# Retention and PReLU MLP on one core: masked scores with q^T, and v with the carried sums, as one product of 128 rows and 64 columns

## The chip, the cores and the metric

The kernel runs on one core of a Trainium2 chip. The metric is the device time of one execution in microseconds. Before the change the median of three runs is 1047.41 us (1045.88 to 1048.51). A profiled execution, which all durations below come from, took 1043.84 us, and its span from the first to the last instruction is 1042.1 us, at a mean granted TensorE clock of 0.997.

## What is computed

Two blocks follow each other. The first is retention: for 8 batches, 8 heads, 576 positions and 64 values a head,

```python
scores = scale * np.matmul(q, k.transpose(0, 1, 3, 2))
gamma = 1.0 - 2.0 ** (-5.0 - np.arange(H, dtype=np.float32))
Dmat = np.where(rel >= 0, gamma[:, None, None] ** rel[None, :, :], 0.0)
ret = scores * Dmat[None, :, :, :]
return np.matmul(ret, v).astype(np.float32)
```

where `rel` is the query's position minus the key's. The result is read as 4608 tokens of 512 values and goes through an MLP, `h = x @ w_in` (512 x 2048), `g = max(h, 0) + alpha * min(h, 0)`, `g @ w_out` (2048 x 512). All data are fp32.

## The kernel before, in words

**Retention in chunks.** The 576 positions of a head are cut into nine chunks of C = 64. A query of chunk j meets the keys of its own chunk through masked scores, and all earlier chunks through one carried sum, a 64x64 matrix of k^T v with its decay. The powers of gamma are put into q and v ahead of the products, so that the mask is only a triangle of ones and a factor for each head. Heads are worked in pairs (c = 0 to 3 in each batch, index n = 4b + c), two heads to the 128 partitions.

For each pair four steps are run, each a function:

- `transposes` (L528): GpSimd multiplies q by its table (L534) and v by its own (`scale`, L512, whose line is L515), and VectorE turns k and q into kT and qT of 64 rows a head, by transposes of 32x32 squares (L539), whose loads `load_sq` lays out so that whole heads come out turned.
- `scores` (L564): 20 products of 64x64 (L573), one head in each half of the rows. VectorE multiplies them by mask and factor (L577) into `at`, in which chunk 2m lies in the lower 64 partitions and chunk 2m + 1 in the upper.
- `states` (L582): 16 products of 64x64 (L588) give k^T v of each chunk but the last; ScalarE copies the even ones (L593), and VectorE adds up the carried sums `su` (L594, L597, L599).
- `values` (L606): 18 products of 64x64 of v with `at` (L612), and 32 of 64 rows by 32 columns of `su` with qT (L619), accumulated in the same PSUM banks. `put_x` (L491) copies the result into the MLP's input blocks with ScalarE (L503, L505); odd chunks lie in exchanged halves and take two copies for each.

**The MLP.** Tokens come in 18 blocks of 256 (kb), the inner dimension in eight slices (i); a pair (kb, i) is a unit. From block 2 on, each unit uses seven products of halves in place of eight: `combine_x` (L420, GpSimd, L427) makes differences of the input, `mlp_unit` (L429) does 14 products of 128x128 by 128 columns (L441); ScalarE copies one of them (L447), VectorE adds (L452), applies the activation (L455, L457) and makes the differences for the second layer (L463); `mlp_out` (L353) does seven products of 256 columns (L361) one unit later. After the last slice `out_block` (L335) adds up the output on VectorE (L347, L348) and stores it.

**Order.** Batch 0 is done in a stage written out by hand while weights are loaded and reduced, batch 1 in the gaps of MLP blocks 0 and 1, whose products are plain (L397, L376). From the third batch on (n = 8 to 31, 24 pairs) the loop at L895 runs `scores`, `states`, the transposes of the next pair and `values`, with units of the queue between them: `cuts` spreads 16 or 24 queued units over the four pairs of a batch, so 4 or 6 go with each pair. One unit lies between states and values in five of the six batches, two in the other. Here the framework's scheduler orders each engine's instructions; each engine runs its own queue in order. The loads of pair n + 1 are issued from SyncE at the start of pair n. Tiles of k, q and v (`nat`) have two buffers each; `kT`, `at` have one, `qT` and `su` two. The products of retention share two PSUM banks (`ps_a`), those of the MLP have two (`ps_h`) and four (`ps_o`).

Of the kernel before, what the change touches and what calls it, by code (L numbers as in the profile page):

```python
# [18 lines left out]
def kernel(  # L19
# [46 lines left out]

    pairs = [(b, c) for b in range(B) for c in range(NPAIR)]

    NEARLY = 2 * NPAIR
# [3 lines left out]
    def load_nat(t, src, b, c):  # L75
        hs, s0 = slice(2 * c, 2 * c + 2), (NM - 1) * P
        for h2 in range(2):
            nc.sync.dma_start(t[:, 0:NM - 1, h2],
                              src[b, 2 * c + h2, 0:s0].rearrange("(m p) d -> p m d", p=P))
        nc.sync.dma_start(t[0:C, NM - 1], src[b, hs, s0:S].rearrange("h p d -> p h d"))  # L80
# [3 lines left out]
    def load_sq(t, src, b, c):  # L84
        for a in range(4):
            f0 = (a % 2) * 32
            nc.sync.dma_start(
                t[32 * a:32 * a + 32],
                src[b, 2 * c + a // 2].rearrange("(n t) d -> t n d", t=32)[:, :, f0:f0 + 32])

    def load_pair(n):
        b, c = pairs[n]
        kn, vn, qx = [nat.tile([P, NM, 2, D], FP32, tag=f"nat_{x}", name=f"{x}n_{n}")
                      for x in "kvq"]
        if n < NEARLY:
            kx = kn
            load_nat(kn, k, b, c)
            load_nat(qx, q, b, c)
        else:
            kx = nat.tile([P, NB, 32], FP32, tag="sq_k", name=f"kx_{n}")  # L100
            qx = qx.rearrange("p m h d -> p (m h d)")[:, 0:S].rearrange(
                "p (n r) -> p n r", r=32)
            load_sq(kx, k, b, c)
            load_sq(qx, q, b, c)
            load_nat(kn, k, b, c)
        load_nat(vn, v, b, c)
        return kn, kx, qx, vn


# [99 lines left out]

    gch = const.tile([P, 3, NPAIR], FP32, name="gch")  # L210
    tabx = const.tile([P, NPAIR, 2], FP32, name="tabx")
    for h2 in range(2):
        hd = slice(h2 * D, (h2 + 1) * D)
        nc.vector.tensor_copy(gch[hd, 0], th[hd, 2, h2:H:2])
        nc.vector.tensor_scalar(tabx[hd, :, 0], pf[hd, 0, h2:H:2], float(D) ** -0.5, None,
                                ALU.mult)
        nc.vector.scalar_tensor_tensor(out=tabx[hd, :, 1], in0=dif[hd, 5, h2:H:2], scalar=1.0,
                                       in1=tabx[hd, :, 0], op0=ALU.add, op1=ALU.mult)
# [301 lines left out]
    def ps_tile(shape, name):  # L520
        return ps_a.tile(shape, FP32, tag="psa", name=name)
# [6 lines left out]
    def transposes(n):  # L528
        c = pairs[n][1]
        kn, kx, qx, vn = loaded[n]  # L530
        kT = attn.tile([P, S], FP32, tag="kT", name=f"kT_{n}")
        qT = attn.tile([P, S], FP32, tag="qT", bufs=2, name=f"qT_{n}")
        qh = qx.rearrange("p (j x) r -> p j x r", x=2)
        nc.gpsimd.tensor_tensor(out=qh, in0=qh,  # L534
                                in1=tabx[:, None, c, :, None].to_broadcast([P, NJ, 2, 32]),
                                op=ALU.mult)
        scale(vn, 1, c)
        for src, dst in ((kx, kT), (qx, qT)):
            nc.vector.transpose(dst, src.rearrange("p n r -> p (n r)"))  # L539
        return kT, qT  # L540

    def turn(n, i):

        src = loaded[n][i]
        dst = attn.tile([P, S], FP32, tag="qT" if i else "kT", bufs=2 if i else 1,
                        name=f"T{i}_{n}")
        for m0, m1 in ((0, 3), (3, NM)):
            w = min(m1 * P, S) - m0 * P
            pt = ps_tile([P, 3 * P], f"pt{i + m0}_{n}")
            for m in range(m0, m1):  # L550
                rows = min(P, S - m * P)
                nc.tensor.transpose(pt[:, (m - m0) * P:(m - m0) * P + rows],  # L552
                                    src[0:rows, m].rearrange("p h d -> p (h d)"),
                                    ident[0:rows, 0:rows])
            nc.scalar.copy(dst[:, m0 * P:m0 * P + w], pt[:, 0:w])
        return dst

    def half(x):
        return slice(x * C, (x + 1) * C)

    def chunk(j):
        return slice(j * C, (j + 1) * C)

    def scores(n, kT, qT):  # L564
        c = pairs[n][1]
        at = attn.tile([P, 2 * NM * C], FP32, tag="at", name=f"at_{n}").rearrange(
            "p (h m s) -> h p m s", h=2, s=C)
        ps = [ps_tile([P, NM, C], f"ps{h2}_{n}") for h2 in range(2)]
        for m in range(NM):
            for p2 in range(2):  # L570
                j = min(2 * m + p2, NJ - 1)
                for h2 in range(2):
                    nc.tensor.matmul(ps[h2][half(p2), m], kT[half(h2), chunk(j)],  # L573
                                     qT[half(h2), chunk(j)], start=True, stop=True)
        for h2 in range(2):
            h = 2 * c + h2
            nc.vector.scalar_tensor_tensor(  # L577
                out=at[h2], in0=ps[h2], scalar=th[:, 3, h:h + 1],
                in1=mask[:, None, :].to_broadcast([P, NM, C]), op0=ALU.mult, op1=ALU.mult)
        return at  # L580

    def states(n, kn, vn):  # L582
        c = pairs[n][1]
        ps = [ps_tile([P, NM - 1, D], f"pu{p2}_{n}") for p2 in range(2)]
        for m in range(NM - 1):
            for p2 in range(2):
                for h2 in range(2):
                    nc.tensor.matmul(ps[p2][half(h2), m], kn[half(p2), m, h2],  # L588
                                     vn[half(p2), m, h2], start=(m == 0), stop=(m == NM - 2),
                                     skip_group_check=True)  # L590
        su = attn.tile([P, NJ - 1, D], FP32, tag="su", bufs=2, name=f"su_{n}")
        g1, g2 = gch[:, 0, c:c + 1], gch[:, 1, c:c + 1]
        nc.scalar.copy(su[:, 0::2], ps[0])  # L593
        nc.vector.scalar_tensor_tensor(out=su[:, 1::2], in0=su[:, 0::2], scalar=g1, in1=ps[1],  # L594
                                       op0=ALU.mult, op1=ALU.add)
        for j in range(3, NJ - 1, 2):
            nc.vector.scalar_tensor_tensor(out=su[:, j], in0=su[:, j - 2], scalar=g2,  # L597
                                           in1=su[:, j], op0=ALU.mult, op1=ALU.add)
        nc.vector.scalar_tensor_tensor(out=su[:, 2::2], in0=su[:, 1:NJ - 3:2], scalar=g1,  # L599
                                       in1=ps[0][:, 1:], op0=ALU.mult, op1=ALU.add)  # L600
        return su
# [4 lines left out]
    def values(n, vn, qT, at, su):  # L606
        b, c = pairs[n]
        pv = [ps_tile([P, NM, C], f"pv{p2}_{n}") for p2 in range(2)]
        for m in range(NM):
            for p2 in range(2 if 2 * m + 1 < NJ else 1):  # L610
                for h2 in range(2):
                    nc.tensor.matmul(pv[p2][half(h2 ^ p2), m], vn[half(p2), m, h2],  # L612
                                     at[h2][half(p2), m], start=(m == 0), stop=False,
                                     skip_group_check=True)
        for j in range(1, NJ):
            for h2 in range(2):
                for e in range(0, D, 32):
                    to = (h2 ^ (j % 2)) * D + e
                    nc.tensor.matmul(pv[j % 2][to:to + 32, j // 2],  # L619
                                     su[half(h2), j - 1, e:e + 32], qT[half(h2), chunk(j)],  # L620
                                     start=False, stop=(j >= NJ - 2), skip_group_check=True)
        for p2 in range(2):
            put_x(b, c, p2, pv[p2])

# [268 lines left out]
    for n, (b, c) in enumerate(pairs):  # L895
        if n < NEARLY:
            continue
        if n + 1 < len(pairs):
            loaded[n + 1] = load_pair(n + 1)
        kn, _, _, vn = loaded[n]  # L900
        share = -(-len(queue) // (NPAIR - c))
        cuts = [(share + i) // 3 for i in range(3)][::-1]
        kT, qT = turned.pop(n) if n in turned else transposes(n)
        at = scores(n, kT, qT)
        pop_units(cuts[0])
        su = states(n, kn, vn)
        pop_units(cuts[1])
        if n + 1 < len(pairs):
            turned[n + 1] = transposes(n + 1)
        values(n, vn, qT, at, su)  # L910
        del loaded[n]
        pop_units(cuts[2])
        if c == NPAIR - 1:
            enqueue(b)
# [31 lines left out]
```

## Time and profile before

| What | from the profile |
|---|---|
| span | 1042.1 us |
| DMA, mean busy share of 16 engines, in tenths | 9 in the first fortieth of the span, 0 to 8 in the next nine, then 1 to 3, 0 in the last eight |
| scores of a pair (L573) | 40 records, mean 223 ns each, overlapped |
| states of a pair (L588) | 32 records, mean 224 ns |
| values of a pair (L612, L619) | 36 records, 223 ns, and 64 records, 224 ns |
| MLP, first layer (L441) | 3584 records, 275 and 278 ns |
| MLP, second layer (L361) | 1792 records, 379 ns |

A record of a matmul is one pass: each fp32 product shows as two passes in the trace, so the 20 products of `scores` are 40 records. The mean duration of a record says how long one pass is in the array, from its first row to its end; passes overlap, so the time that a group takes is read from the chain of work that ended last, not from the mean. A few matmul records can be missing from a trace. In the groups, "64*32" after a name is the part of the array that the product used, rows by columns.

### The profile page before, as it was taken

The numbers are of one execution on the slowest core, as the hardware profiler recorded it, in microseconds if no ns is written. First come the engines' busy times: TensorE is split into PE (matmuls) and PEld (weight loads), VectorE is DVE, ScalarE is ACT, GpSimd is POOL, SyncE is SP. The second block draws the span as 40 slices with busy tenths as digits, with TensorE's granted clock in tenths as the row PEclk, the third lists the DMA queues.
The fourth block names the chain that finished last, engine by engine and source line by source line (L and its number), as shares of the span: only waits on it lengthen the run. The fifth ranks groups of instructions, "written<-read, shape, count | busy, mean of one in ns | idle before, by whom it ended". The sixth has DMA issues, their size and how long they took to land.

```text
span 1042.1 us, 27067 instructions
## 1 busy us (share of the span) xinstructions
PE 1024.3 (98%) x11329; PEld 902.0 (87%) x11329; DVE 748.2 (72%) x1951; ACT 170.8 (16%) x533; POOL 214.8 (21%) x253
## 2 busy tenths in 40 slices
PE   5999999999999999999999999999999999999998
PEld 4766667999999999999999999999999999999997
DVE  7766755776786778776768777867777776766675
ACT  4545532111111110110110011111111111000000
POOL 4566675411301020200011111301030001010000
PEclk8999999999999999999999999999999999999999
DMA  9855605233232221121212232222222100000000
GB/s 244 252 153 139 163 20 122 41 68 64 48 67 45 59 47 44 35 56 24 56 36 50 42 68 46 57 47 53 62 40 52 24 22 2 21 1 22 1 21 21
DMA packets 216073, 63.36 MB, mean 61 GB/s; under 512 B 201088, under 2 KB 209296, under 8 KB 215952
## 3 DMA queue, kind: packets, MB, share of 16 engines
q1 hardware_dynamic: 213840, 61.11, 25.3%
q8 instruction: 89, 1.46, 0.6%
q10 hardware_dynamic: 2112, 0.53, 0.3%
q14 instruction: 32, 0.26, 0.1%
HBM read 52.17 MB, written 9.44 MB: 59 GB/s over the span
## 4 chain that ended last, share of the span: by engine, by line
PE 97%; DMA 1%; issue 1%; POOL 0%; DVE 0%; ACT 0%; SPq 0%; DVEq 0%; POOLq 0%
PE ph L441 40%; PE po L361 37%; PE ph L397 6%; PE po L376 5%; PE pv L619 2%; PE ps L573 2%; PE pv L612 2%; PE pu L588 2%; DMA w_out<-in_k_dram 1%; PE pt L552 0%; PE pt L653 0%; PE pv L726 0%; PE ps L672 0%; PE pv L715 0%; POOL w_out L304 0%
## 5 line engine op out<-in xcount | busy, mean ns | idle before, releaser
L361 PE MATMUL po<-w_out,g 128*128 128x256 f32 x1792 | 407.8, 379 | 0.0
L361 PEld LDWEIGHTS po<-w_out,g 128*128 128x128 f32 x1792 | 330.8, 190 | 39.7
L452 DVE TENSOR_TENSOR g<-ph,g 128x256 f32<-128x256 f32 (+1 forms) x512 | 187.4, 387 | 176.6 <-PE ph L441 95.7
L441 PE MATMUL ph<-xb,w_in 128*128 128x128 f32 x2048 | 277.6, 278 | 0.0
L441 PEld LDWEIGHTS ph<-xb,w_in 128*128 128x128 f32 x2048 | 253.2, 192 | 9.2 <-issue 0.7
L441 PE MATMUL ph<-xt,w_in 128*128 128x128 f32 x1536 | 213.6, 275 | 0.0
L441 PEld LDWEIGHTS ph<-xt,w_in 128*128 128x128 f32 x1536 | 192.2, 192 | 0.1
L463 DVE TENSOR_TENSOR g<-g 128x128 f32<-128x128 f32 x512 | 143.0, 320 | 7.8
L447 ACT COPY g<-ph 128x128 f32<-128x128 f32 x128 | 34.0, 265 | 462.2 <-PE ph L441 457.3
L515 POOL TENSOR_TENSOR vn<-vn,th 128x512 f32<-128x512 f32 (+1 forms) x56 | 39.7, 729 | 336.0 <-DMA vn<-in_v_dram 315.2
L455 DVE TENSOR_SCALAR g<-g,alpha 128x256 f32<-128x256 f32 x256 | 92.1, 402 | 4.5
L457 DVE SCALAR_TENSOR_TENSOR g<-g 128x512 f32<-128x512 f32 x128 | 91.8, 717 | 3.8
L397 PE MATMUL ph<-xb,w_in 128*128 128x256 f32 x256 | 61.1, 394 | 1.1 <-ACT xb L733 1.1
L427 POOL TENSOR_TENSOR xt<-xb,xt 128x256 f32<-128x256 f32 x32 | 25.2, 788 | 172.3 <-ACT xb L505 163.3
L376 PE MATMUL po<-w_out,g 128*128 128x512 f32 x128 | 59.0, 604 | 0.1
L397 PEld LDWEIGHTS ph<-xb,w_in 128*128 128x128 f32 x256 | 49.2, 196 | 10.0 <-issue 2.4
L503 ACT COPY xb<-pv 64x64 f32<-64x64 f32 (+1 forms) x144 | 33.9, 236 | 145.7 <-PE pv L619 143.9
L376 PEld LDWEIGHTS po<-w_out,g 128*128 128x128 f32 x128 | 23.1, 190 | 24.3 <-issue 22.5
L539 DVE STREAM_TRANSPOSE qT<-qn 128x576 f32<-128x576 f32 x24 | 18.7, 778 | 28.9 <-PE pv L619 23.1
L413 DVE SCALAR_TENSOR_TENSOR g<-g,nalpha,ph 128x256 f32<-128x256 f32 x32 | 13.9, 477 | 31.6 <-ACT ph L403 31.6
L534 POOL TENSOR_TENSOR qn<-qn,tabx 128x576 f32<-128x576 f32 x24 | 28.1, 1171 | 28.7 <-DMA qn<-in_q_dram 22.8
L427 POOL TENSOR_TENSOR xt<-xb 128x256 f32<-128x256 f32 x16 | 11.5, 722 | 107.3 <-PE ph L441 107.3
(127 smaller groups left out, 665.0 us busy)
## 6 DMA issues: line engine op xcount, KB each, us to landing
out_dram<-osb SPq DMA_DIRECT2D x36, 256.0 KB, 2.2
kn<-in_k_dram SPq DMA_DIRECT2D x56, 128.0 KB, 2.9
vn<-in_v_dram SPq DMA_DIRECT2D x56, 128.0 KB, 2.8
kx<-in_k_dram SPq DMA_DIRECT2D x96, 72.0 KB, 2.5
qn<-in_q_dram SPq DMA_DIRECT2D x96, 72.0 KB, 2.6
raw<-in_moe_w_in_dram SPq DMA_DIRECT2D x24, 256.0 KB, 4.2
raw<-in_moe_w_out_dram SPq DMA_DIRECT2D x10, 512.0 KB, 4.5
w_in<-in_moe_w_out_dram SPq DMA_DIRECT2D x6, 512.0 KB, 4.8
```

What stands on the lines that cost most here:

```text
L361: nc.tensor.matmul(acc[kb][n // 2][:, n % 2, :], g[:, x, :], w_out[i][:, y, :], start=(i == 0 and n % 2 == 0), stop=(i == NU - 1 and (n % ...
L376: nc.tensor.matmul(acc[kb][m], g[:, 2 * x + m], w_out[i][:, 2 * x:2 * x + 2].rearrange("p x f -> p (x f)"), start=(i == 0 and x == 0), sto ...
L397: nc.tensor.matmul(ph[:, x], w_in[i // UST][:, cc // 2 * 2 + x, i % UST, cc % 2], xb[kb][:, cc], start=(cc == 0 and x == 0), stop=(cc == N ...
L427: nc.gpsimd.tensor_tensor(out=o, in0=x0, in1=x1, op=ALU.subtract)
L441: nc.tensor.matmul(ph[m][:, o], w_in[i // UST][:, l, i % UST, cc], r[:, cc], start=(n in (0, 3) and cc == 0), stop=(n in (2, 6) and cc == ...
L447: nc.scalar.copy(g[:, 7], ph[0][:, 2])
L452: nc.vector.tensor_tensor(out=o, in0=x0, in1=x1, op=ALU.add)
L455: nc.vector.tensor_scalar(g[:, 4 + 2 * m:6 + 2 * m], g[:, 2 * m:2 * m + 2], 0.0, alpha[:, fc:fc + 1], ALU.min, ALU.mult)
L457: nc.vector.scalar_tensor_tensor(out=g[:, 0:4].rearrange("p x t -> p (x t)"), in0=g[:, 0:4].rearrange("p x t -> p (x t)"), scalar=0.0, in1 ...
L463: ins = nc.vector.tensor_tensor(out=g[:, o, :], in0=g[:, x0, :], in1=g[:, x1, :], op=op)
L503: nc.scalar.copy(to[half(h2)], pv[half(1 - h2), m:m + n])
L515: nc.gpsimd.tensor_tensor(out=t[0:rows, m], in0=t[0:rows, m], in1=th[0:rows, x, None, 2 * c:2 * c + 2, None].to_broadcast([rows, n, 2, D]) ...
```

## The change

From the third batch on, v and the carried sums of a head are put into one matrix of 128 rows for each chunk, and the masked scores and q^T into another, so that one product gives a chunk's values of one head. In the tile of v, head h2 has v in the partitions of the other half (`half(1 - h2)`) and the carried sums in its own half; the first chunk has zeros there, set by GpSimd. In the tile `mt`, head h2 has masked scores in the other half and its q^T in its own. So `pair_values` has 18 products of 128 rows, 64 columns of the array and 64 columns of data, without accumulation, and head h2 comes out in the half of the PSUM partitions that it has in the MLP's input. ScalarE copies q^T into `mt` and the sums into v's tile, and it now multiplies v by its table, which GpSimd did. `pair_scores` has 18 products in place of 20, its mask takes four operations of 64 partitions, `pair_states` has two for the odd sums. The functions `scores`, `states` and `values` stay for the pairs of batch 1.

Besides, k (as the states need it) and v are loaded with the positions of a chunk in 64 partitions, two loads each in place of three; the sums of the new pairs lie in kT's buffer, those of batch 1 in that of k's squares; qT has one buffer; and the transposes of pair 8 come ahead of the loads of pair 9 and behind one MLP unit, which leaves 15 of the 16 units to that batch's `cuts`. The core of the diff:

```diff
     def load_pair(n):
...
-            load_nat(kn, k, b, c)
-        load_nat(vn, v, b, c)
+            kn = kn[:, 0:S].rearrange("p (j d) -> p j d", d=D)
+            vn = vn.rearrange("p (h j d) -> p h j d", h=2, d=D)
+            for h2 in range(2):
+                load_head(kn[half(1 - h2)], k, b, 2 * c + h2)
+                load_head(vn[half(1 - h2), h2], v, b, 2 * c + h2)
+
+                nc.gpsimd.memset(vn[half(h2), h2, 0], 0.0)
...
     def transposes(n):
...
-        qT = attn.tile([P, S], FP32, tag="qT", bufs=2, name=f"qT_{n}")
+        qT = attn.tile([P, S], FP32, tag="qT", name=f"qT_{n}")
...
-        scale(vn, 1, c)
+        for h2 in range(2):
+            x = half(1 - h2)
+            nc.scalar.activation(vn[x, h2], vn[x, h2], ACTF.Copy, scale=tabv[x, c:c + 1])
...
     def states(n, kn, vn):
...
-        su = attn.tile([P, NJ - 1, D], FP32, tag="su", bufs=2, name=f"su_{n}")
+        su = nat.tile([P, S], FP32, tag="sq_k", name=f"su_{n}")[:, 0:S - D].rearrange(
+            "p (j d) -> p j d", d=D)
...
+    def pair_scores(n, kT, qT):
...
+        ps = [ps_tile([P, NM, C], f"ps{p2}_{n}") for p2 in range(2)]
+        for j in range(NJ):
+            for h2 in range(2):
+                x = (1 - h2, h2)[j % 2]
+                nc.tensor.matmul(ps[j % 2][half(x), j // 2], kT[half(h2), chunk(j)],
+                                 qT[half(h2), chunk(j)], start=True, stop=True)
+        for h2 in range(2):
+            nc.scalar.copy(mt[half(h2), h2].rearrange("p j s -> p (j s)"), qT[half(h2)])
+        for p2 in range(2):
+            for h2 in range(2):
+                h, to, x = 2 * c + h2, half(1 - h2), (1 - h2, h2)[p2]
+                nm = NM - p2
+                nc.vector.scalar_tensor_tensor(
+                    out=mt[to, h2, p2::2], in0=ps[p2][half(x), 0:nm], scalar=th[to, 3, h:h + 1],
+                    in1=mask[to, None, :].to_broadcast([C, nm, C]), op0=ALU.mult, op1=ALU.mult)
+        return mt
+
+    def pair_states(n, kn, vn):
...
+        su = attn.tile([P, S], FP32, tag="kT", name=f"su_{n}")[:, 0:S - D].rearrange(
+            "p (j d) -> p j d", d=D)
+        g1, g2 = gch[:, 0, c:c + 1], gch[:, 1, c:c + 1]
+        nc.scalar.copy(su[:, 0::2], ps[0])
+        for h2 in range(2):
+            nc.vector.scalar_tensor_tensor(
+                out=su[half(h2), 1::2], in0=su[half(h2), 0::2], scalar=g1[half(h2)],
+                in1=ps[1][half(1 - h2)], op0=ALU.mult, op1=ALU.add)
...
+        for h2 in range(2):
+            nc.scalar.copy(vn[half(h2), h2, 1:], su[half(h2)])
+
+    def pair_values(n, vn, mt):
...
+        j1 = -b * NJ % w or w
+        j1 += w if NJ - j1 > 6 else 0
+        pv = [ps_tile([P, (j1, NJ - j1)[i], C], f"pv{i}_{n}") for i in range(2)]
+        for j in range(NJ):
+            for h2 in range(2):
+                nc.tensor.matmul(pv[j >= j1][half(h2), j - (j1 if j >= j1 else 0)],
+                                 vn[:, h2, j], mt[:, h2, j], start=True, stop=True)
...
+            m, i = min(w - o, NJ - j), j >= j1
+            j0 = j - (j1 if i else 0)
+            nc.scalar.copy(xb[kb][:, c, o * C:(o + m) * C].rearrange("p (j s) -> p j s", s=C),
+                           pv[i][:, j0:j0 + m])
...
+        if n == NEARLY:
+            pop_units(1)
+            turned[n] = transposes(n)
         if n + 1 < len(pairs):
             loaded[n + 1] = load_pair(n + 1)
...
-        kT, qT = turned.pop(n) if n in turned else transposes(n)
-        at = scores(n, kT, qT)
+        kT, qT = turned.pop(n)
+        mt = pair_scores(n, kT, qT)
         pop_units(cuts[0])
-        su = states(n, kn, vn)
+        pair_states(n, kn, vn)
         pop_units(cuts[1])
         if n + 1 < len(pairs):
             turned[n + 1] = transposes(n + 1)
-        values(n, vn, qT, at, su)
+        pair_values(n, vn, mt)
```

More of the change, by code (lines that the diff above doesn't have):

```diff
@@ L67, with half @@
     pairs = [(b, c) for b in range(B) for c in range(NPAIR)]
+    def half(x):
+        return slice(x * C, (x + 1) * C)
     NEARLY = 2 * NPAIR
@@ L89, in load_sq, with load_head @@
                 src[b, 2 * c + a // 2].rearrange("(n t) d -> t n d", t=32)[:, :, f0:f0 + 32])
+    def load_head(t, src, b, h):
+        nc.sync.dma_start(t, src[b, h].rearrange("(j t) d -> t j d", t=C))
     def load_pair(n):
         b, c = pairs[n]
-        kn, vn, qx = [nat.tile([P, NM, 2, D], FP32, tag=f"nat_{x}", name=f"{x}n_{n}")
-                      for x in "kvq"]
+        kn = nat.tile([P, NM * P], FP32, tag="nat_k", name=f"kn_{n}")
+        qx = nat.tile([P, NM * P], FP32, tag="nat_q", name=f"qn_{n}")
+        vn = nat.tile([P, 2 * S], FP32, tag="nat_v", name=f"vn_{n}")
         if n < NEARLY:
+            kn, qx, vn = [t[:, 0:NM * P].rearrange("p (m h d) -> p m h d", h=2, d=D)
+                          for t in (kn, qx, vn)]
             kx = kn
@@ L98, in load_pair @@
             load_nat(qx, q, b, c)
+            load_nat(vn, v, b, c)
         else:
-            kx = nat.tile([P, NB, 32], FP32, tag="sq_k", name=f"kx_{n}")
-            qx = qx.rearrange("p m h d -> p (m h d)")[:, 0:S].rearrange(
+            kx = nat.tile([P, S], FP32, tag="sq_k", name=f"kx_{n}").rearrange(
                 "p (n r) -> p n r", r=32)
+            qx = qx[:, 0:S].rearrange("p (n r) -> p n r", r=32)
             load_sq(kx, k, b, c)
             load_sq(qx, q, b, c)
-            load_nat(kn, k, b, c)
-        load_nat(vn, v, b, c)
+            kn = kn[:, 0:S].rearrange("p (j d) -> p j d", d=D)
[4 more added lines that the diff above has]
+                nc.gpsimd.memset(vn[half(h2), h2, 0], 0.0)
         return kn, kx, qx, vn
@@ L211 @@
     tabx = const.tile([P, NPAIR, 2], FP32, name="tabx")
+    tabv = const.tile([P, NPAIR], FP32, name="tabv")
     for h2 in range(2):
         hd = slice(h2 * D, (h2 + 1) * D)
+        nc.vector.tensor_copy(tabv[half(1 - h2)], th[half(1 - h2), 1, h2:H:2])
         nc.vector.tensor_copy(gch[hd, 0], th[hd, 2, h2:H:2])
@@ L544, in turn @@
         src = loaded[n][i]
-        dst = attn.tile([P, S], FP32, tag="qT" if i else "kT", bufs=2 if i else 1,
-                        name=f"T{i}_{n}")
+        dst = attn.tile([P, S], FP32, tag="qT" if i else "kT", name=f"T{i}_{n}")
         for m0, m1 in ((0, 3), (3, NM)):
@@ L556, in turn @@
         return dst
-    def half(x):
-        return slice(x * C, (x + 1) * C)
     def chunk(j):
@@ L565, in scores @@
         c = pairs[n][1]
-        at = attn.tile([P, 2 * NM * C], FP32, tag="at", name=f"at_{n}").rearrange(
+        at = attn.tile([P, 2 * S], FP32, tag="at", name=f"at_{n}")[:, 0:2 * NM * C].rearrange(
             "p (h m s) -> h p m s", h=2, s=C)
@@ L623, in values @@
             put_x(b, c, p2, pv[p2])
+    def pair_scores(n, kT, qT):
+        c = pairs[n][1]
+        mt = attn.tile([P, 2 * S], FP32, tag="at", name=f"mt_{n}").rearrange(
+            "p (h j s) -> p h j s", h=2, s=C)
+        ps = [ps_tile([P, NM, C], f"ps{p2}_{n}") for p2 in range(2)]
[14 more added lines that the diff above has]
+        return mt
@@ new lines, in pair_states @@
+    def pair_states(n, kn, vn):
+        c = pairs[n][1]
+        ps = [ps_tile([P, NM - 1, D], f"pu{p2}_{n}") for p2 in range(2)]
+        for j in range(NJ - 1):
+            for h2 in range(2):
+                x = (h2, 1 - h2)[j % 2]
+                nc.tensor.matmul(ps[j % 2][half(x), j // 2], kn[half(1 - h2), j],
+                                 vn[half(1 - h2), h2, j], start=True, stop=True)
+        su = attn.tile([P, S], FP32, tag="kT", name=f"su_{n}")[:, 0:S - D].rearrange(
[6 more added lines that the diff above has]
+                in1=ps[1][half(1 - h2)], op0=ALU.mult, op1=ALU.add)
+        for j in range(3, NJ - 1, 2):
+            nc.vector.scalar_tensor_tensor(out=su[:, j], in0=su[:, j - 2], scalar=g2,
+                                           in1=su[:, j], op0=ALU.mult, op1=ALU.add)
+        nc.vector.scalar_tensor_tensor(out=su[:, 2::2], in0=su[:, 1:NJ - 3:2], scalar=g1,
+                                       in1=ps[0][:, 1:], op0=ALU.mult, op1=ALU.add)
+        for h2 in range(2):
+            nc.scalar.copy(vn[half(h2), h2, 1:], su[half(h2)])
@@ new lines, in pair_values @@
+    def pair_values(n, vn, mt):
+        b, c = pairs[n]
+        w = TB // C
+        j1 = -b * NJ % w or w
+        j1 += w if NJ - j1 > 6 else 0
+        pv = [ps_tile([P, (j1, NJ - j1)[i], C], f"pv{i}_{n}") for i in range(2)]
+        for j in range(NJ):
+            for h2 in range(2):
+                nc.tensor.matmul(pv[j >= j1][half(h2), j - (j1 if j >= j1 else 0)],
+                                 vn[:, h2, j], mt[:, h2, j], start=True, stop=True)
+        j = 0
+        while j < NJ:
+            kb, o = divmod(b * NJ + j, w)
+            if kb not in xb:
+                xb[kb] = ring.tile([P, NCC, TB], FP32, tag=f"x{kb % NRING}", name=f"xb_{kb}")
+            m, i = min(w - o, NJ - j), j >= j1
+            j0 = j - (j1 if i else 0)
+            nc.scalar.copy(xb[kb][:, c, o * C:(o + m) * C].rearrange("p (j s) -> p j s", s=C),
+                           pv[i][:, j0:j0 + m])
+            j += m
```

## The prediction

> **What bounds the kernel now.** I read the busy shares first, then who ended the waits of TensorE, then the chain that ended last. The busy shares (the columns are busy time, share of the span, instructions):
>
> ```profile
> PE 1024.3 (98%) x11329; PEld 902.0 (87%) x11329; DVE 748.2 (72%) x1951; ACT 170.8 (16%) x533; POOL 214.8 (21%) x253
> ```
>
> A busy TensorE alone proves little, so the waits of its matmuls come next (the columns are total, times, longest, in us):
>
> ```profile
> PE pt L653 <- DMA w_out<-in_k_dram: 6.1, 2, 5.0
> ...
> PE ps L573 <- DVE qT L539: 2.3, 1, 2.3
> ```
>
> Nearly all waiting lies in the first stage, which the diff leaves alone. From the third batch on there is one wait, 2.3 us, where the first `scores` of the loop (L573) wait for the transposed q. The chain that ended last, one pair of heads from 402 to 430 us (start, length, what; matmuls and weight loads counted together):
>
> ```profile
> 402.25 0.62 PE pu L588 x32
> 402.87 3.32 PE ph L441 x28
> 406.19 3.02 PE po L361 x14
> 409.22 3.12 PE ph L441 x28
> 412.34 3.02 PE po L361 x14
> 415.37 0.73 PE pv L612 x36
> 416.09 0.79 PE pv L619 x53
> 416.88 3.32 PE ph L441 x28
> 420.20 3.02 PE po L361 x14
> 423.23 3.12 PE ph L441 x28
> 426.35 3.02 PE po L361 x14
> 429.38 0.74 PE ps L573 x40
> ```
>
> Piece follows piece with no other engine between them. In the trace these lengths repeat for all 24 pairs: states (L588) 0.62, values (L612 and L619) 0.73 + 0.79 = 1.52, scores (L573) 0.74 us. So the time is the sum of TensorE's pieces; another engine counts only if it makes TensorE wait.
>
> **Rates from the same view.** Each fp32 product is two passes in the trace (L441 has 14 products a unit, 28 records). 28 passes of 128 columns last 3.12 us, 0.111 each; 14 of 256 columns 3.02 us, 0.216 each. In scores, passes of 64 columns start in fours about 7 ns apart, one per 64x64 quarter of the array, and the next four start 58 ns later: a slot of 58.3 ns carries four passes. 40 passes are ten slots, 0.583 us, so 0.74 leaves 0.159 us for filling and emptying; 32 passes are eight slots, 0.466, and 0.62 leaves the same. A further 94 ns lie before the first pass and 101 ns behind the phase's first MLP pass.
>
> **What the Trainium skill says.** "TensorEngine Tiling (Array Packing)", "Available Configurations" and "Key Properties": 64x64 gives four tiles, 64x32 eight, 128x64 two; tiles load and multiply in parallel; a change of tiling drains the engine. The first agrees with the fours 7 ns apart, the last with the 94 and 101 ns and with a gap of 68 ns between L612 and L619. No 128x64 product is in the trace. "PSUM — Partial Sum Buffer", "PSUM bank collisions raise a hardware error": two row tiles must not write one bank in the same quadrant (32 partitions); different quadrants of a bank may be used at once. L619 already writes one bank from both row halves, into different column halves, and its first 32 passes start within 0.24 us. "ScalarE: Activation LUTs", "What ACT_TABLE_LOAD costs": with immediate operands 186 ns + 0.833 ns an element, 93 ns more for a scale read from a column.
>
> **The change, part by part** (24 pairs, from the third batch on).
>
> 1. Values. Removed: 18 products of 64x64 and 32 of 64x32, 1.52 us. Added: 18 products of 128 rows by 64 columns, whose column halves are h2 = 0 and 1. They are 36 passes in two tiles, so 18 slots if the two overlap as the four did: 18 x 0.0583 = 1.049, plus 0.159 = 1.208 us. Saved 0.31 x 24 = **7.4 us**. Bounds: if the halves don't overlap, 36 x 0.0583 + 0.159 = 2.258, a loss of 0.74 x 24 = 17.7; if the 0.159 vanished too, a gain of 11.3. I take overlap: in scores the two column halves of one row half already stream different data at once.
>
> 2. Scores go from 20 products to 18. A quarter with five products still needs ten slots; L612 also has 18 products, and its last passes start 0.58 us after its first, as with 20. Nothing. States stay at 16 products, eight slots. Both now have two row halves in one bank, always in opposite column halves, as in L619: zero; had the row halves to take turns, slots would double, (0.58 + 0.47) x 24 = 25 us, which L619's first half excludes.
>
> 3. Start of the loop. The transposes of the first pair move ahead of its scores, behind one MLP unit. In the new program order a whole L441 block (3.1 us) and the last four products of the plain blocks stand before those scores, against a part of that block now. The 2.3 us wait disappears: **2.3 us**. Bounds 0 and 2.3.
>
> 4. VectorE. The mask becomes four operations, two of 320 and two of 256 columns (0.544 and 0.48 us, rows L577 and L594) instead of two of 320: +0.96 us a pair. The odd sums take two operations of 64 rows instead of one of 128 at the same 0.48: +0.48. Together 1.44 x 24 = 35 us, 72% to 75%. Hidden: a unit gives VectorE 4.0 us of work in TensorE's 6.14; PSUM banks of a unit are wanted again 3.0 us after its L441 ends. After a scores phase the four masks end about 2.4 us later, when the unit's second bank is just being filled (3.1). Cost 0, upper bound 2 us in all for blocks that also drain an output (seven L347/L348 of 0.42).
>
> 5. ScalarE. Added: two scalings of v (64x576, by the page 186 + 93 + 480 = 759 ns, an estimate; row L278 has 677 for 512), two copies of q^T (64x576) and two of the sums (64x512; row L733 has 580 for that shape): about 3.9 us. The xb copies fall from about eight to three, 1.9 to 1.0 us. Net some 3 us a pair, ScalarE from 16% to 23%: hidden, as it idles up to 6 us between operations. Its queue is in order: the scalings wait for v of the next pair, whose load starts when the values two pairs back release the buffer. At 600.19 us TensorE left L619, and at 603.19 the multiplication of v on GpSimd began, so the load takes 3 us. ScalarE then stands for 3 to 4.5 us after values; behind it is the copy L447 of the next unit but one, wanted 7 us after values. Hidden.
>
> 6. GpSimd loses two L515 a pair (1.04 + 0.42 us) and gets two clears of 64x64 (L166: 0.15 for 128x64). The clears wait for the buffer of v, too; behind them stand L534 and `combine_x` of blocks several units away. Nothing. SyncE issues 12 loads a pair in place of 14 with the same bytes; the DMA engines are mostly idle after the first quarter. The sums now borrow kT's buffer and the early pairs' sums kx's: in the new order kT's next transpose follows the copies, and the first loads wait once for a transpose that nothing urgent follows.
>
> 7. New wait: values need the sums copied into v. Before, the last sum (L599) ends 2.26 us after states in most pairs, 4.41 at worst, and values start 6.28 us after states where one unit lies between (20 pairs), 12.4 in the other four. Added: 0.48 (odd sums), 0.42 (an L452 put between the sums) and 1.25 (the copies): 4.4, at worst 6.6. Slack 1.9 us typically, and 0.3 us lost in a bad case: 0 to 0.5 in all.
>
> **Sum.** 7.4 + 2.3 = 9.7 us. Against the profiled span of 1042.1 that is 1032.4. That span is 5.3 us below the median of the timed runs (1047.41; they lie between 1045.88 and 1048.51), so I forecast 1047.4 - 9.7 = **1037.7 us**, or 0.9% less. About 0.3%, 3.1 us, can be told from no change.
>
> **Rivals.** *The column halves take turns (slower).* For it: 128 rows use every row of the array, and no trace shows two such tiles at once. Against it: scores do it with half the rows. Time: 1047.4 + 17.7 - 2.3 = 1062.8. It decides from the slot upwards: even is where 18 slots cost 1.361 + 2.3/24 = 1.457 us, at 81 ns a slot instead of 58. Chance 0.10. *The copies of the sums take the place of the matmuls saved.* For it: ScalarE's queue and the VectorE operations put between the sums; against it: 1.9 us of slack. If each of the 20 tight pairs waits 0.4 us, 8 us come back: 1045.7. Chance 0.08, half of it under 1044.3. *More than forecast:* the fill of a values phase shrinks, as the second change of tile shape is gone: 0.15 x 24 = 3.6 us, 1034.1. Chance 0.05. The forecast itself has 0.77; its own range, 1035 to 1041, is timing scatter and parts 3, 4 and 7.
>
> **Numbers.** Faster: 0.77 + 0.05 + 0.04 = 0.86; within 0.3%: 0.04; slower: 0.10. The range 1034 to 1044.5 takes in the second case of more gain and half of the waiting one, and leaves out about 0.16.
>
> **What would show it.** In the chain after: a values piece of 1.21 us with 36 passes in slots of 58 ns; scores 0.74 and states 0.62 as now; no PE wait for qT; MLP pieces of 3.12 and 3.02 without gaps. Wrong: a values piece of 2.2 us or slots near 117 ns (halves in turn); PE waiting for ACT vn (the copies) or for VectorE's masks; pieces of L441 longer than 3.32 (PSUM not freed in time).

## The result and the profile after

The changed kernel takes 1036.57 us (median of four runs, 1035.70 to 1037.36), against 1046.91 us for four runs of the kernel before: 10.3 us less, a ratio of 0.990 with a 95% interval of 0.9882 to 0.9917. A later comparison of the same kernel gave 1036.31 us and 0.9908 (0.9893 to 0.9923). The forecast was 1037.7.

The busy shares of the kernel after (busy time, share of the span, instructions):

```profile
PE 1017.0 (98%) x9697; PEld 896.4 (87%) x9697; DVE 758.2 (73%) x2025; ACT 247.8 (24%) x557; POOL 186.2 (18%) x253
```

TensorE stays at 98% and has 7.3 us less to do, with 1632 fewer passes (68 in each of 24 pairs). VectorE's share hardly moves, ScalarE gains 77 us, GpSimd loses 29. Whether any of this matters is in the waits of TensorE's matmuls (total, times, longest, us):

```profile
PE pt L742 <- DMA w_out<-in_k_dram: 6.0, 2, 4.7
...
PE pv L701 <- ACT vn L690: 0.3, 1, 0.3
```

The wait for qT is gone. In its place stands one that names the copies of the sums (L690) as the last thing that the first pair's values (L701) wait for. The chain that ended last, over the same kind of pair as before (start, length, what):

```profile
412.14 1.20 PE pv L701 x36
413.34 3.32 PE ph L461 x28
416.67 3.02 PE po L381 x14
419.69 3.12 PE ph L461 x28
422.81 3.02 PE po L381 x14
425.84 0.73 PE ps L655 x36
426.56 3.32 PE ph L461 x28
...
439.06 0.62 PE pu L674 x32
```

Values are one piece of 1.20 us where there were two of 0.73 and 0.79; scores, states and the MLP pieces last as before, and no other engine appears between them. (L461 and L381 are the MLP's layers, L441 and L361 before; L655, L674 and L701 are `pair_scores`, `pair_states`, `pair_values`.)

For the comparisons below I call the stretch from the first pass of a halved MLP unit (L441, L461) to the end of the span the **loop**, and a piece of retention with the two changes of tile shape around it (94 + 101 ns) its **cost**. The loop takes 880.61 us before and 871.27 after, 9.34 less. Phase by phase, from the trace: values cost 1.711 before and 1.394 after in 23 of the 24 pairs, 23 x 0.317 = 7.3 us; the first pair costs 2.356, as it waits 0.96, so it takes back 0.65; scores cost 0.937 and 0.924, 0.3 us in all; states 0.820 in both; the wait for qT gives 2.3. That is 9.2 us of the 9.34. The remaining 1.0 us of the timed 10.3 is not placed. It isn't in the two traces, whose stage ahead of the loop is 0.85 us longer after (161.52 and 162.37 us); over all traces that stage varies from 161.5 to 164.9 us, and the four timed runs of each kernel scatter by 2.6 and 1.7 us.

### The profile page after: what moved, and what is told of

It reads as the page before. It is cut to its first block, busy times and chain, and to the rows that moved or that the text cites. A ratio compares the mean times of both kernels' runs of the same rounds, so it can differ in the third digit from the quotient of the medians.

```text
span 1033.6 us, 23754 instructions
## 1 busy us (share of the span) xinstructions
PE 1017.0 (98%) x9697; PEld 896.4 (87%) x9697; DVE 758.2 (73%) x2025; ACT 247.8 (24%) x557; POOL 186.2 (18%) x253
## 4 chain that ended last, share of the span: by engine, by line
PE 95%; DVE 2%; POOL 1%; issue 1%; DMA 1%; ACT 1%; SPq 0%; DVEq 0%; POOLq 0%; ACTq 0%
PE ph L461 39%; PE po L381 36%; PE ph L417 6%; PE po L396 5%; PE pv L701 3%; PE ps L655 2%; PE pu L674 1%; DMA w_out<-in_k_dram 1%; PE pt L573 0%; PE pt L742 0%; DVE g L472 0%; PE pv L638 0%; PE ps L761 0%; PE ps L591 0%; PE pv L631 0%
## 5 line engine op out<-in xcount | busy, mean ns | idle before, releaser
L381 PE MATMUL po<-w_out,g 128*128 128x256 f32 x1792 | 407.8, 379 | 0.0
L381 PEld LDWEIGHTS po<-w_out,g 128*128 128x128 f32 x1792 | 330.8, 190 | 39.7
L472 DVE TENSOR_TENSOR g<-ph,g 128x256 f32<-128x256 f32 (+1 forms) x512 | 187.3, 387 | 178.7 <-ACT g L467 95.8
L461 PE MATMUL ph<-xb,w_in 128*128 128x128 f32 x2048 | 277.7, 279 | 0.0
L461 PEld LDWEIGHTS ph<-xb,w_in 128*128 128x128 f32 x2048 | 253.1, 192 | 8.2 <-issue 0.5
L461 PE MATMUL ph<-xt,w_in 128*128 128x128 f32 x1536 | 213.3, 275 | 0.0
L461 PEld LDWEIGHTS ph<-xt,w_in 128*128 128x128 f32 x1536 | 192.1, 192 | 0.0
L483 DVE TENSOR_TENSOR g<-g 128x128 f32<-128x128 f32 x512 | 128.5, 292 | 7.8
L475 DVE TENSOR_SCALAR g<-g,alpha 128x256 f32<-128x256 f32 x256 | 84.1, 370 | 3.7
L554 POOL TENSOR_TENSOR qn<-qn,tabx 128x576 f32<-128x576 f32 x24 | 28.2, 1173 | 217.3 <-DMA qn<-in_q_dram 174.7
L663 DVE SCALAR_TENSOR_TENSOR mt<-ps,th,mask 64x256 f32<-64x256 f32 (+1 forms) x96 | 49.5, 516 | 4.0 <-PE ps L655 2.7
L559 ACT ACTIVATE vn<-vn,tabv 64x576 f32<-64x576 f32 x48 | 37.1, 773 | 28.5 <-DMA vn<-in_v_dram 27.8
L124 POOL MEMSET vn<- 64x64 f32 x48 | 7.0, 146 | 194.0 <-PE pv L701 113.5
L710 ACT COPY xb<-pv 128x256 f32<-128x256 f32 (+3 forms) x72 | 19.7, 323 | 78.1 <-PE pv L701 78.1
L679 ACT COPY su<-pu 128x256 f32<-128x256 f32 x24 | 8.9, 373 | 122.4 <-PE pu L674 122.4
```

The source lines that it names most:

```text
L381: nc.tensor.matmul(acc[kb][n // 2][:, n % 2, :], g[:, x, :], w_out[i][:, y, :], start=(i == 0 and n % 2 == 0), stop=(i == NU - 1 and (n % ...
L461: nc.tensor.matmul(ph[m][:, o], w_in[i // UST][:, l, i % UST, cc], r[:, cc], start=(n in (0, 3) and cc == 0), stop=(n in (2, 6) and cc == ...
L472: nc.vector.tensor_tensor(out=o, in0=x0, in1=x1, op=ALU.add)
L475: nc.vector.tensor_scalar(g[:, 4 + 2 * m:6 + 2 * m], g[:, 2 * m:2 * m + 2], 0.0, alpha[:, fc:fc + 1], ALU.min, ALU.mult)
L483: ins = nc.vector.tensor_tensor(out=g[:, o, :], in0=g[:, x0, :], in1=g[:, x1, :], op=op)
L559: nc.scalar.activation(vn[x, h2], vn[x, h2], ACTF.Copy, scale=tabv[x, c:c + 1])
```

## The experiments

All ratios are against the kernel before, run beside them. Where two versions of the changed kernel differ by less than their intervals, I compare the loops in their traces: the changed kernel profiled twice gave 871.27 and 871.28.

### One part alone: the early transposes

The kernel before, with its first transposes moved as in the change:

```diff
         if n < NEARLY:
             continue
+        if n == NEARLY:
+            pop_units(1)
+            turned[n] = transposes(n)
```

> Only the move of the first pair's transposes behind one MLP unit is added to the kernel before. Slot theory (the time is the sum of TensorE's pieces, and the move takes away one wait): the 2.3 us wait of the first scores for qT goes, all pieces of the pairs stay at 0.74, 0.62 and 1.52 us, so the span falls by 2.3 us and the time by about 0.2%. Rival (the move makes up most of the gain, since later pairs start better prepared): a fall of 5 us or more. Rival (the wait only changes its place): no fall.

It took 1042.86 us, ratio 0.9969 (0.9956 to 0.9981); its loop is 878.28, 2.33 less than before (the timed medians differ by 3.6 us, with an interval from 2.0 to 4.6). The chain of this kernel at the start of the loop shows why (start, length, what):

```profile
163.02 3.12 PE ph L441 x28
166.15 3.44 PE po L376 x8
169.58 0.74 PE ps L573 x40
```

Scores follow the plain MLP block at once. Step 3 was worth its 2.3 us.

### The column halves

The changed kernel, with all products of one column half ahead of those of the other:

```diff
-        for j in range(NJ):
-            for h2 in range(2):
+        for h2 in range(2):
+            for j in range(NJ):
```

> The changed kernel with its 18 products of values in another order: first all nine of one head (one column half), then all nine of the other, so that neighbours never lie in different halves. Same products, same data. Slot theory (two column halves share a slot of 58 ns): 36 slots in place of 18, a values piece of 2.25 us in place of 1.20, and 24 x 1.05 = 25 us more than the changed kernel, about 1062 us. Rival (TensorE reorders far enough ahead, or each pass costs 33 ns whatever its place): unchanged at about 1036.6 us.

It took 1058.04 us, ratio 1.0099 (1.0075 to 1.0123), slower than the kernel before, with the same products and the same data. Its chain, at the same pair:

```profile
417.92 3.02 PE po L381 x14
420.94 2.06 PE pv L701 x36
423.00 3.32 PE ph L461 x28
```

The 36 passes of values last 2.06 us in place of 1.20, and 24 x 0.86 = 20.7 us, less 0.65 because the first pair now waits 0.31 us in place of 0.96, is the whole growth of the loop (20.1). That is less than the 25 us expected. The starts of single passes tell the mechanism: in the changed kernel they come in twos 6.6 ns apart, the next two 58.3 ns later; here one starts every 58.3 ns. The time is 0.2 us short of 36 slots for a reason that is in the same list: from 421.74 us on, three starts come 4 or 5 ns behind another (421.738 and .743, .850 and .854, .908 and .913), so 33 slots are needed, 33 x 0.0583 + 0.159 = 2.08. The records don't name the column half. By their pace (the second start 107 ns behind the first, then one every 58.3 ns) the starts at .743, .850 and .908 are the first three of the second half, and that at .913 is the last of the first half. TensorE therefore takes up a product of the other column half ahead of its turn, at most three passes ahead; "each engine runs its own queue in order" holds for it only to within these few passes. Products of different columns overlap if they stand next to each other in the program.

### The rows

The same products over the 64 rows of v and masked scores alone. The carried sums are left out of the output, so the products do only the chunk's own part:

```diff
-                                 vn[:, h2, j], mt[:, h2, j], start=True, stop=True)
+                                 vn[half(1 - h2), h2, j], mt[half(1 - h2), h2, j],
+                                 start=True, stop=True)
```

> The changed kernel with products of values over the 64 rows that hold v and the masked scores alone; the carried sums are left out of the output. Slot theory (a pass costs its 64 columns of data, and rows are free): the values piece stays at 1.20 us and the time within 0.2% of the changed kernel. Rival (the 128 rows cost something: a longer load of weights or a longer drain): the piece falls by 0.1 us or more, the time by 2.4 us or more.

It took 1036.13 us, ratio 0.9902 (0.9881 to 0.9924). The chain at the same pair:

```profile
412.15 1.19 PE pv L701 x36
413.34 2.76 PE ph L461 x23
```

1.19 against 1.20 us: in these products the second 64 rows, all the work of the carried sums, cost nothing that can be seen. That doesn't make rows free in general. These 18 products use two of the four quarters of the array and leave the other two idle; L612 before spreads 18 products of 64 rows over all four and takes 0.73 us. The loop is 1.04 us shorter; 0.96 of that is the first pair's wait, which is gone because these products don't read the copied sums.

### The first pair's wait

Where do 0.96 us come from, when pairs later on have two to spare? The timeline of the kernel after, at the first pair (start, length, engine, line, operation; in brackets the idle time before it and what ended it):

```profile
178.85 2.61 POOL L324 TENSOR_TENSOR w_in<-w_in 128x512 f32<-128x512 f32 x2
...
181.41 1.15 POOL L554 TENSOR_TENSOR qn<-qn,tabx 128x576 f32<-128x576 f32 x1
...
182.60 0.78 DVE L561 STREAM_TRANSPOSE qT<-qn 128x576 f32<-128x576 f32 x1 [2.19 <-POOL qn L554]
...
182.97 0.37 ACT L679 COPY su<-pu 128x256 f32<-128x256 f32 x1 [4.32 <-PE pu L674]
...
185.69 0.97 DVE L681 SCALAR_TENSOR_TENSOR su<-su,gch,pu 64x256 f32<-64x256 f32 x2
```

GpSimd is still combining weights (L324, 1.27 us each) from the stage ahead, so its product of the next pair's q and the table (L554) is late. The transpose of that q (L561) is next in VectorE's queue and holds it for 2.2 us with nothing done; the MLP's activation and then the sums stand behind it. The first of the sums (L681) starts 2.35 us after the copy that it needs has ended. As the trace reads, the wait named after ScalarE's copies is thus GpSimd's: the chain that leads to the values passes through L324 and L554 (L324 itself was released by VectorE's L483 of an earlier unit), and its end reads

```profile
188.99 0.62 ACT vn L690
...
189.63 0.62 ACT vn L690
...
190.30 1.15 PE pv L701 x30
```

I gave the first pair a second unit ahead of its values:

```diff
         cuts = [(share + i) // 3 for i in range(3)][::-1]
+        if n == NEARLY:
+            cuts = [1, 2, 1]
```

> The changed kernel with the first pair's units cut 1, 2, 1 in place of 2, 1, 1: two MLP units lie between its states and its values. In the changed kernel the values of that pair wait about 0.96 us for the copies of the sums, which end 7.3 us after states. Slot theory: the wait goes, nothing else changes, span 1.0 us shorter (about 0.1%, at the edge of what the timing tells; the trace decides). Rival (the copies are late because of something in front of them that moves along with the units): the wait stays.

It took 1036.78 us, ratio 0.9902 (0.9879 to 0.9925), and the loop is 0.16 us shorter, not 1.0: the rival of the expectation held. The wait of the values is gone, but VectorE still stands for GpSimd, and the unit put there takes the delay instead; the waits of this kernel name it:

```profile
PE ph L461 <- DVE g L472: 0.6, 1, 0.6
```

So the delay is moved, not removed: a second unit ahead of values doesn't help while VectorE's queue itself is held. No run takes work away from GpSimd at this place; a run below gives it more, and the wait grows by 1.4 us.

### The copies of the sums

To see how near the new wait is in the other 23 pairs, the copies are made twice and three times:

```diff
-        for h2 in range(2):
+        for h2 in (0, 1, 0, 1):
             nc.scalar.copy(vn[half(h2), h2, 1:], su[half(h2)])
```

> The changed kernel with the two copies of the sums into v done twice (four ScalarE copies a pair). In the changed kernel the copies end 4.25 us after states and values start 6.28 us after. Slot theory with that slack: they now end at 5.5 us, still in time, so nothing but the first pair (1.3 us more wait) changes: 0 to 1.5 us slower. Rival (ScalarE's queue already delays the MLP's copies): 1.3 us for each pair, up to 30 us.

> As the one before, with the copies done three times (six a pair). Slot theory with 2.0 us of slack: they end 6.8 us after states, 0.55 us late in the 19 pairs with one unit between, so 10.5 us, plus 2.6 us for the first pair: about 13 us slower than the changed kernel. Rival (more slack than the trace shows): no change. Rival (queue delays): much more than 13 us.

Twice: 1037.98 us, ratio 0.9914 (0.9883 to 0.9945). The loop grows by 3.2 us, more than the 0 to 1.5 expected: some 1.95 in the first pair, 1.4 in MLP pieces that wait, which the expectation put at nothing; all other pairs still cost 1.394. Three times: 1049.78 us, ratio 1.003 (1.0019 to 1.0040), loop +12.2. Here the waiting pairs show; the chain of the kernel with three copies, at one of them:

```profile
297.22 0.62 ACT vn L690
...
297.86 0.63 ACT vn L690
...
298.50 0.63 ACT vn L690
...
299.17 1.15 PE pv L701 x30
```

Median cost of values 1.865, 0.47 more, except in the batch with two units ahead of values, where it stays 1.394. In the changed kernel the copies end 4.25 us after states and values start at 6.28: 2.0 us to spare. Two more pairs of copies would move the end to 6.82, 0.54 us too late, which agrees with 0.47. Step 7's slack is real, and its limit lies between one and two further pairs of copies.

### Who multiplies v

In the changed kernel, v goes back to GpSimd:

```diff
-            nc.scalar.activation(vn[x, h2], vn[x, h2], ACTF.Copy, scale=tabv[x, c:c + 1])
+            nc.gpsimd.tensor_tensor(out=vn[x, h2], in0=vn[x, h2],
+                                    in1=tabv[x, c:c + 1, None].to_broadcast([C, NJ, D]),
+                                    op=ALU.mult)
```

> The changed kernel with v multiplied by its table on GpSimd, as before, in place of ScalarE. Slot theory: both engines have room, no TensorE wait appears, the time stays within 0.2% of the changed kernel. Rival (part of the gain comes from taking this work off GpSimd, whose two-input operations hold up VectorE): slower by 2 us or more, with longer VectorE operations beside it and TensorE waiting for them.

It took 1039.65 us, ratio 0.9923 (0.9899 to 0.9948). The loop is 3.4 us longer: the first pair's values wait 1.4 us more, and MLP pieces wait 1.9 us in all. So GpSimd didn't have the room that the expectation gave it, and its rival held. The groups (busy time, mean ns of one, idle time before) show a second effect. First the kernel after, then the one with v on GpSimd, then the kernel before, whose L463 and L455 are the same two operations:

```profile
L483 DVE TENSOR_TENSOR g<-g 128x128 f32<-128x128 f32 x512 | 128.5, 292 | 7.8
...
L475 DVE TENSOR_SCALAR g<-g,alpha 128x256 f32<-128x256 f32 x256 | 84.1, 370 | 3.7
```

```profile
L483 DVE TENSOR_TENSOR g<-g 128x128 f32<-128x128 f32 x512 | 136.4, 308 | 7.8
...
L475 DVE TENSOR_SCALAR g<-g,alpha 128x256 f32<-128x256 f32 x256 | 101.7, 439 | 3.6
```

```profile
L463 DVE TENSOR_TENSOR g<-g 128x128 f32<-128x128 f32 x512 | 143.0, 320 | 7.8
...
L455 DVE TENSOR_SCALAR g<-g,alpha 128x256 f32<-128x256 f32 x256 | 92.1, 402 | 4.5
```

GpSimd is busy for 90 us of the loop after, 148 with v on GpSimd (64 partitions at a time take it 1195 ns each, 57 us in all, more than the 35 us of the form before), and 119 before. The second group's mean follows this, the first group's doesn't: it is longest before. The single operations show why. Of the 512 of the first group, 9, 27 and 28 (in the order of the views) overlap in time with an operation of GpSimd, and these last 571, 669 and 894 ns in the mean; no other lasts more than 294 ns, and the mean of the others is 287 or 288 ns in all three kernels. Of the 256 of the second group, 17, 51 and 40 overlap, with means of 715, 815 and 680 ns; the others have 346, 346 and 350. So what counts is how many operations meet one of GpSimd's, and for how long, not GpSimd's total. "SBUF — State Buffer", "Who interferes with whom", in the Trainium skill, says that VectorE operations in a 2-port mode, or with two inputs in SBUF, share a port pair with GpSimd and that the later one waits. The single operations agree, and so does L472, which has one input in PSUM: after, its mean is 387 ns with an overlap and without.

### A further version: scores and states as one piece

If a phase pays 0.159 us of filling and emptying and 0.195 of shape changes whatever it holds, then joining two phases should save 0.354 us a pair, or 0.412 if a slot of 58 ns goes too, as the expectation has it. States need no result of the scores, and both are 64x64, so one function runs them in succession, in two banks (the last chunk's scores in a bank of `ps_h`), with the units split in two instead of three (the function itself, `pair_front`, isn't shown):

```diff
-        cuts = [(share + i) // 3 for i in range(3)][::-1]
+        cuts = share - share // 2, share // 2
...
-        mt = pair_scores(n, kT, qT)
+        mt = pair_front(n, kT, qT, kn, vn)
         pop_units(cuts[0])
-        pair_states(n, kn, vn)
-        pop_units(cuts[1])
```

> A further step: scores and states of a pair are one phase of 64x64 products, with one filling and one emptying in place of two. The PSUM banks are shared out anew (chunk 8's scores in a bank of the MLP's first layer), the units of a pair are split in two in place of three. Slot theory: a phase costs 0.354 us beside its slots, and 34 products in four quarters need 17 slots in place of 10 + 8: 24 x (0.354 + 0.058) = 9.9 us, plus 1.0 us of the first pair's wait: about 1025.7 us. Rival (VectorE's burst of masks and sums behind the one phase holds up the MLP's PSUM banks): the gain is eaten by waits of L461, 1030 to 1040 us.

It took 1030.63 us, ratio 0.9839 (0.9813 to 0.9865). The joined piece costs 1.390 us against 0.924 + 0.820, a saving of 0.354, or 8.5 us for 24 pairs. The further slot was miscounted: of 34 products two quarters of the array get nine each, which is 18 slots, as many as ten and eight. The wait of the first pair's values is gone as well, but the loop is only 5.2 us shorter, and the time lies in the rival's range. TensorE waits 3.9 us in MLP pieces; the chain of this kernel at the largest of these waits:

```profile
226.79 0.34 DVE s L367
227.12 0.66 DVE osb L367 x2
227.78 0.33 DVE osb L368
...
228.15 0.29 DVE mt L711
...
228.45 0.29 DVE mt L711
...
228.78 2.05 PE ph L461 x16
```

The output of a token block (L367, L368) is drained on VectorE just ahead of the mask of the last chunk (L711), and the next unit waits for the bank that this mask reads. Both come from the position of the units, so I shifted them by two against the pairs:

```diff
         if n == NEARLY:
-            pop_units(1)
+            pop_units(2)
             turned[n] = transposes(n)
...
-        share = -(-len(queue) // (NPAIR - c))
+        share = -(-(len(queue) - 2) // (NPAIR - c))
```

> The kernel with one front a pair, its units moved by two (two MLP units ahead of the first pair, and two left in the queue at the end of each batch), so that the front's masks and sums and the seven operations that drain an output block no longer meet on VectorE. In the kernel with one front, TensorE stood for some 3.9 us in the MLP's pieces, mostly where both met. Theory (the meeting causes the waits): most of them go, and the stretch from the first L461 to the end falls from 866.1 to about 863 us, the time to about 1027.5 us. Rival (the front's burst alone is too long for the banks): the waits stay at about 3.9 us.

> The changed kernel once more, on the same chip as the run beside it, for a comparison of times: about 1036.6 us, and a stretch from the first L461 to the end of 871.3 us.

The shifted version took 1027.10 us, ratio 0.9822 (0.9805 to 0.9839); beside it the changed kernel took 1036.31. Its loop is 862.18 us, 9.1 less than the changed kernel's: 24 x 0.354 = 8.5 and the first pair's 0.96, less 0.4 us because more time lies behind TensorE's last pass (5.06 us against 4.64). Its chain:

```profile
405.94 3.02 PE po L381 x14
408.96 0.20 PE pl L701 x2
...
409.23 0.46 PE ps L701 x27
409.69 0.47 PE ps L707 x32
410.16 3.32 PE ph L461 x28
```

Scores (L701) and states (L707) run through without a gap, and from the third batch on TensorE waits for no other engine. This version is faster than both kernels.

## Why the prediction was right, step by step

1. **Values** (7.4 us): right. The piece was to be 1.208 us and is 1.20; saved 0.317 a pair against 0.308. The choice between the two bounds, that the column halves overlap, was the whole risk, and the products in the other order show it: something near the slower rival happens when neighbours use the same columns. As "TensorEngine Tiling (Array Packing)", "Available Configurations", has it, 128x64 gives two tiles, and here two passes share a slot of 58.3 ns. What the step doesn't say is that no slot was saved. L612 has ten, and L619's 64 passes, eight to a slot as its first 32 start (within 0.238 us), would have eight: 18 together, as many as the new products. By the starts of passes, the piece before is 0.580 (L612) + 0.148 to L619 + 0.642 (L619) + 0.146 to the MLP = 1.516 us, the piece after 1.047 + 0.152 = 1.198. Eight slots of states lie 0.477 us from first start to last, so L619 takes 0.165 more than its slots, all of it behind its first 32 passes; the other 0.153 is about one filling and emptying (0.159). The gain is thus two phases made one, and an uneven phase gone. Why L619 is uneven, no run shows, nor whether the same sums as 64x64 products in the phase of L612 would have saved as much.
2. **Scores and states** (nothing): right, 0.3 us of gain in scores, none in states. Two row halves in one bank, in different quadrants, cost nothing: 0.73 us where separate banks took 0.74, and 0.62 in both.
3. **Start** (2.3 us): right, shown alone at 2.33.
4. **VectorE** (hidden): right about the path, wrong about the load. It was to grow by 35 us and grew by 10 in the loop (641.8 to 651.8). The added operations are there; the two groups above, which the change doesn't touch, fell by 14.5 and 8.0 us. The step priced VectorE's operations as if they didn't depend on GpSimd. That the error went the harmless way was luck; whether 35 us more would have stayed hidden, no run shows.
5. **ScalarE** (hidden): right. The scaling of v was put at 759 ns with the figures of "ScalarE: Activation LUTs", "What ACT_TABLE_LOAD costs", and measures 773.
6. **GpSimd** ("Nothing"): mis-sized. Taking v away from it is worth about 3 us against leaving it there, in the form that was run (57 us of GpSimd's time; with the 35 us of the form before it may be less, which no run shows): in the first pair, where GpSimd is late, and in MLP pieces behind VectorE. As that is a loss avoided, it doesn't appear as a gain against the kernel before.
7. **The new wait** (0 to 0.5 us in all): mis-sized, at 0.96. The size for the usual pair was right (copies were to end 4.4 us after states, and end at 4.25). The worst case was taken from the pairs of the kernel before (6.6); the first pair has 7.31. By the trace that is because its next transposes now stand in VectorE's queue ahead of the sums and wait for a late GpSimd, which no pair of before showed.

The sum was 9.7 us; the loop gave 9.34 and the timed medians 10.3. The rival of the waiting copies is true of one pair in 24. The rival of a smaller fill doesn't hold: 1.20 - 18 x 0.0583 = 0.15 us, as in the other phases.

## What to carry to other kernels

Where TensorE's pieces follow each other without a gap, count slots and phases. In these runs small fp32 products share a slot when they use different parts of the array (four of 64x64, or two of 128x64) and stand next to each other in the program. Filling the rows with a second sum didn't lower the number of slots; it made one phase out of two. Each phase of another tile shape between MLP pieces pays its filling, emptying and shape changes again, here 0.35 us, so join phases before trimming products in them. When work is taken from GpSimd or given to it, measure VectorE again, and read a wait's releaser back along its queue: what is named last need not be what was late.

## What the runs showed of the hardware beyond this

- 18 products of 128 rows by 64 columns took no longer than 18 of 64 rows in the same two column halves, one row half each (1.20 and 1.19 us); 18 of 64 rows spread over all four quarters took 0.73 us.
- Products of the other column half started up to three passes ahead of their place in the program; beyond that the order of the program decided (2.06 us against 1.20).
- The means of two groups of VectorE operations differed by up to 19% between kernels (370 to 439 ns for 128x256, 292 to 320 ns for 128x128); those that overlapped no operation of GpSimd took the same in all (346 to 350 and 287 to 288 ns).
